# Attention and gated MoE on one core: transposes of q and x through the DMA crossbar, batch loads held behind them, and a regrouped opening

## The chip, the cores and the metric

The kernel runs on one core of a Trainium2 chip. The metric is the device time of one execution in microseconds (us). The core has five engines that run their own instruction streams in order and wait for each other through semaphores: TensorE (PE, matmuls and transposes, with its weight loads shown as PEld), VectorE (DVE), ScalarE (ACT), GpSimd (POOL) and SyncE (SP). SP and POOL also issue DMA transfers, each from its own queue. PSUM, where matmuls put their results, is used in 8 buffers, four for each of two pools.

## The reference

There are 8 batches of 8 heads, 576 tokens and 64 channels a head. Attention is linear, then normalised by head and token; the gated feed-forward block works on 4608 tokens of 512 channels, with 1536 hidden columns:

```python
kv = np.einsum('bhsd,bhse->bhde', k, v)
out = np.einsum('bhsd,bhde->bhse', q, kv)
rms = np.sqrt(np.mean(out * out, axis=-1, keepdims=True) + 1e-06)
x = (out / rms * g_norm)            # then [B, S, H*D] as 4608 x 512
g = x @ w_gate
gelu = 0.5 * g * (1.0 + erf(g * inv_sqrt2))
val = x @ w_val
ffn_out = gelu * val @ w_out
res_gate = 1.0 / (1.0 + np.exp(-(x @ w_res)))
return x + res_gate * ffn_out
```

## The kernel before, in words

Work goes by blocks. Blocks 0 to 7 hold the first 512 tokens of batches 0 to 7, as 4 groups (j) of 128 tokens; block 8 gathers the last 64 tokens of all batches, two batches to a group. All matmuls take fp16 and sum in fp32.

A MoE block has 12 slots of `m_gval` (one hidden tile f each: 4 matmuls `gps` with the gate weights, 4 matmuls `vps` with the value weights, N = 512, then gelu on ACT and the product `hid` on DVE) and 4 slots of `m_out` (one group j each: 4 matmuls `rps` for the gate of the residual, 12 matmuls `fps` over the hidden tiles, then `pf` and `osb` on DVE and a store from SP). Both `gps` and `vps` need x with its channels on the partitions, the tile `xT`; `m_out` adds x itself, the tile `t`. Block 0 is in another form: its first two hidden tiles are made group by group while the attention of batch 0 is finished, and its outputs run over f for all four groups at once (`out_by_f`).

The attention of batch b = m + 1 is woven into the slots of block m, by the table in `attn_plan`: `by_token` (L106, DVE) puts q and k into token order; `a_qT` transposes q with 16 PE transposes (L151) that ACT copies out of PSUM (L152); `a_kv` makes k'v with 20 matmuls (L161, L168); `a_o` makes the output with 16 matmuls (L190); ACT squares it (L183), DVE sums (L184), `a_norm` finds 1/rms on DVE, `a_t` (L248) scales into `t`; `a_xT` transposes that with 16 PE transposes (L260) which ACT copies out with the factor g (L261); `a_x` (L267, DVE) multiplies `t` itself by g. Odd batches also do the last 64 tokens of two batches: 4 more transposes of q (`a_rem_qT`, L200), `a_rem_o`, and 4 more of x. Six of the seven such batches, 2 to 7, run in blocks 1 to 6; the attention of batch 1 runs in block 0.

`load_batch` issues six cast transfers (fp32 in HBM to fp16 in SBUF) on POOL's queue. Its call stands in the second slot of a block, and the transfer of q waits until `by_token` has read the buffer. The order on each engine is the order in which the program calls; nothing is rescheduled.

The opening loads q, k and v of batch 0 as fp32 in two halves of four heads on SP's queue, casts them on ACT, DVE and POOL, and runs the attention of batch 0 by half (`f_...` functions). `keep_warm` issues matmuls on zeros, whose result is not used. The weights follow on POOL's queue.

Of the kernel before, what the change touches and what calls it, by code (L numbers as in the profile page):

```python
# [18 lines left out]
def kernel(  # L19
# [15 lines left out]
    nc = tc.nc  # L35
# [96 lines left out]
    def new_block(blk):  # L132
        pool, kw = (xp, {}) if blk < B else (consts, {})
        t_t[blk] = pool.tile([P, NJ, C], FP16, tag="t" if blk < B else "tl", name="t")
        xT_t[blk] = pool.tile([P, NP, NJ * P], FP16, tag="xT" if blk < B else "xTl", name="xT")
# [119 lines left out]
    def a_xT(b, j):  # L255

        blk, jj = where(b, j)
        ps = pattn.tile([P, NP, P], FP16, tag="at", name="xtp")
        for cc in range(NP):
            nc.tensor.transpose(ps[:, cc, :], t_t[blk][:, jj, cc * P : (cc + 1) * P], ident)  # L260
        nc.scalar.activation(  # L261
            out=xT_t[blk][:, :, jj * P : (jj + 1) * P], in_=ps, func=AF.Copy, scale=gcol
        )

    def a_x(b, j):
        blk, jj = where(b, j)
        nc.vector.tensor_tensor(out=t_t[blk][:, jj, :], in0=t_t[blk][:, jj, :], in1=g16, op=ALU.mult)  # L267

# [14 lines left out]
    def m_mm(ps, ws, f, blk, j0, j1):  # L283
        w = w_of(ws, f)
        for cc in range(NP):
# [3 lines left out]
                rhs=xT_t[blk][:, cc, j0 * P : j1 * P],  # L289
                start=(cc == 0),  # L290
                stop=(cc == NP - 1),
# [11 lines left out]
    def m_gval_first(blk, after):  # L303

        hids[blk] = hidp.tile([P, NF, NJ * P], FP16, tag="hid", name="hid")
        tiles = [pmoe.tile([P, NJ * P], FP32, tag="mm", name=n) for n in ("gps", "vps", "gps", "vps")]
        for j in range(NJ):
            after(j)
            for f in range(2):
                m_mm(tiles[2 * f], wg_c, f, blk, j, j + 1)  # L310
                m_mm(tiles[2 * f + 1], wv_c, f, blk, j, j + 1)
        for f in range(2):
            m_act(blk, f, tiles[2 * f], tiles[2 * f + 1])

    def m_res(blk, j):
        rps = pmoe.tile([P, C], FP32, tag="mm", name="rps")
        for cc in range(NP):
            nc.tensor.matmul(  # L318
                rps,
                lhsT=xT_t[blk][:, cc, j * P : (j + 1) * P],  # L320
# [58 lines left out]
    for which in "kv":  # L379
        t = hidp.tile([P, NF, NJ * P], FP16, tag="hid", name=which + "f")  # L380
        t = t.rearrange("p a b -> p (a b)").bitcast(FP32)[:, 0 : H * NJ * D]
        raw[0, which] = t.rearrange("p (h x) -> p h x", h=H)
    for half in range(2):
        lo, hi = half * HH, (half + 1) * HH
        for which, t in (("q", q), ("k", k), ("v", v)):
            nc.sync.dma_start(out=raw[0, which][:, lo:hi, :], in_=rows4(t, 0, lo, hi))
# [5 lines left out]
    load_last_kv(0)  # L392
    ident32 = consts.tile([P, P], FP32, name="ident32")
    make_identity(nc, ident32)

# [34 lines left out]
    def f_cast(which, half, copy):  # L430
        hs = slice(half * HH, (half + 1) * HH)
        dst, src = b16_t[0, which], raw[0, which]
        if which == "v":
            copy(out=dst[:, hs, :], in_=src[:, hs, :])  # L434
        else:
            copy(
                out=dst.rearrange("p j h d -> p h j d")[:, hs, :, :],
                in_=src.rearrange("p h (j d) -> p h j d", j=NJ)[:, hs, :, :],
            )
# [55 lines left out]

    def f_t(half, j0, n):
        hs = slice(half * HH, (half + 1) * HH)
        ps = first["o", half, j0]
        nc.vector.reciprocal(out=rinv0[:, j0 : j0 + n, hs], in_=rms0[:, j0 : j0 + n, hs])
# [8 lines left out]
    def f_xT(half, j0, n, pool, tag):  # L508
        first["xT", half, j0] = ps = pool.tile([P, 2, n, P], FP16, tag=tag, name="xtp")
# [4 lines left out]

    def f_xT_out(half, j0, n, on_vector):
        ps = first["xT", half, j0]
        dst = xT0[:, 2 * half : 2 * half + 2, j0 * P : (j0 + n) * P].rearrange("p c (j t) -> p c j t", j=n)
# [6 lines left out]
    f_cast("q", 0, nc.scalar.copy)  # L524
    f_cast("k", 0, nc.vector.tensor_copy)
    f_qT(0)
    f_qT_out(0, nc.scalar.copy)
    f_qT_out(1, nc.vector.tensor_copy)
    f_cast("v", 0, nc.gpsimd.tensor_copy)
    keep_warm(3)  # L530
    f_kv(0)
    f_kv_out(0)
    f_cast("q", 1, nc.scalar.copy)
    f_o(0, 0, 2, pmoe, "mm")
    f_o(0, 2, 2, pmoe, "mm")
    f_sq(0, 0, 2)
    f_red(0, 0, 2)
    f_qT(1)
    f_qT_out(2, nc.scalar.copy)
    f_qT_out(3, nc.vector.tensor_copy)  # L540
    f_cast("k", 1, nc.gpsimd.tensor_copy)
    for i in range(len(WCS)):
        load_wgv(i)
    load_qr(0)
    f_sqrt(0, 0, 2)
    f_t(0, 0, 2)
    f_sq(0, 2, 2)
    f_red(0, 2, 2)
    f_sqrt(0, 2, 2)
    keep_warm(8)  # L550
    f_cast("v", 1, nc.vector.tensor_copy)
# [3 lines left out]
    f_xT_out(0, 0, 2, False)  # L555
    f_t(0, 2, 2)
    for j in range(NJ):
        f_o(1, j, 1, pattn, "at")
    f_sq(1, 0, 1)
    f_sq(1, 1, 1)  # L560
    f_red(1, 0, 1)
    f_sqrt(1, 0, 1)
    f_t(1, 0, 1)
    keep_warm(2)
    f_xT(0, 2, 2, pmoe, "mm")
    f_sq(1, 2, 1)
    f_xT(1, 0, 1, pattn, "at")
    f_xT_out(1, 0, 1, False)
    f_red(1, 1, 1)
    f_sqrt(1, 1, 1)  # L570
    f_t(1, 1, 1)
    f_xT_out(0, 2, 2, False)
    f_sq(1, 3, 1)
    f_red(1, 2, 1)

    def first_chunk(j):

        if j == 1:
            f_xT(1, 1, 1, pattn, "at")
            f_xT_out(1, 1, 1, False)  # L580
            f_sqrt(1, 2, 1)
            f_t(1, 2, 1)
            f_red(1, 3, 1)
        elif j == 2:
            f_xT(1, 2, 1, pattn, "at")
            f_sqrt(1, 3, 1)
            f_xT_out(1, 2, 1, False)
            f_t(1, 3, 1)
            nc.scalar.preload_act_table_set("gelu_and_others")
        elif j == 3:  # L590
            f_xT(1, 3, 1, pattn, "at")
            f_xT_out(1, 3, 1, True)

            nc.vector.memset(ones16, 1.0)
            nc.vector.tensor_copy(out=grow16, in_=grow[:, None, :].to_broadcast([1, H, D]))
            for t in last_kv[1]:
                nc.vector.memset(t[R:P], 0.0)
            for t in qtr:
                nc.vector.memset(t, 0.0)
# [8 lines left out]
    def attn_plan(b):  # L608
        odd = b % 2 == 1
# [3 lines left out]
        y = [lambda j=j: a_x(b, j) for j in range(NJ + 1)]  # L613
        return [
            [lambda: by_token(b, "q"), lambda: by_token(b, "k")],
            [lambda: attn_begin(b), lambda: a_qT(b, 0)] + ([lambda: load_batch(b + 1)] if b + 1 < B else []),
            [lambda: a_qT(b, 1), lambda: a_kv(b, 0, 2)],
            [lambda: a_kv(b, 2, 4)] + ([lambda: a_rem_qT(b)] if odd else []),
            [o[0]] + ([lambda: a_rem_o(b)] if odd else []),
            [o[1]],  # L620
            [o[2]],
            [o[3]],
            [lambda: a_norm(b), t[0], t[1]],
            [t[2], t[3]],
            [t[4]] if odd else [],
            [],
            [x[0], x[1]],
            [x[2], x[3], y[0], y[1]],
            ([x[4]] if odd else []) + [y[2], y[3]],
            [y[4]] if odd else [],  # L630
        ]

    late = []
    for blk in range(B + 1):
        plan = {}
# [28 lines left out]
        if blk == 0:  # L664
            late = stores
# [30 lines left out]
```

## Time and profile before

| | |
|---|---|
| Time, median of 3 runs | 375.41 us (374.79 to 377.87) |
| The profiled execution | 375.42 us, of which the span of instructions is 373.6 us |
| Mean granted TensorE clock | 0.993 |
| PE busy | 358.0 us, 96% of the span |
| DVE, ACT, POOL busy | 215.6, 153.2 and 47.0 us |
| HBM read, written | 38.80 MB, 9.44 MB |
| Issue of a 512 KB batch load of q, k, v to its landing, median | 6.0, 7.9 and 9.8 us |

In rows of the profile, `L260 PE MATMUL xtp<-ident,t` is line 260 of the kernel before, on PE, which writes tile xtp and reads ident and t. A time in brackets is how long the engine sat idle before the row, and behind the arrow stands what ended that. Matmuls are pipelined, so the busy time of one (0.38 us at N = 512) is longer than the distance from one to the next; the distance is read from the starts in the timeline. In rows of windows, the columns are the window, its length, the busy time of PE, PEld, DVE, ACT and POOL with the number of instructions, the granted clock, the mean busy share of the DMA engines, and GB/s.

### The profile page before, as it was taken

Reading aid. Unit: us, or ns where it says so; the run is one execution under the profiler, and the core shown is the slowest. Engines: PE = TensorE matmul, PEld = TensorE weight load, DVE = VectorE, ACT = ScalarE, POOL = GpSimd, SP = SyncE. Lnnn points to the kernel's source line nnn. Section 1 sums busy time; section 2 is a strip of 40 time slices with the busy share of each in tenths; the row PEclk is TensorE's granted clock in tenths of the full one; section 3 lists DMA queues with packets and bytes.
Section 4 is the critical chain, followed back from the end, with each engine's and each line's share of the span. In section 5 each row is a group of like instructions: output and inputs, shape, how many; then the busy total and the mean of one; then the engine's idle time right before and its main releaser. Section 6 shows DMA issues by size and latency. Waiting matters only on the chain.

```text
span 373.6 us, 5442 instructions
## 1 busy us (share of the span) xinstructions
PE 358.0 (96%) x2120; PEld 180.6 (48%) x2120; DVE 215.6 (58%) x427; ACT 153.2 (41%) x257; POOL 47.0 (13%) x65
## 2 busy tenths in 40 slices
PE   6779999999999999999999999999999999999993
PEld 2554464554455455545464445444644444444441
DVE  2566448778546946584657664756478453343422
ACT  3563373453346344544364335533563333123310
POOL 3843140500050002200130005000000000000000
PEclk9899999999999999999999999999999999999998
DMA  9999997590159012901192029601000200020013
GB/s 246 187 202 197 198 200 74 81 221 2 58 107 141 0 56 63 182 5 56 61 172 18 28 84 133 58 31 56 30 0 2 84 29 2 28 80 7 0 43 70
DMA packets 49452, 30.76 MB, mean 82 GB/s; under 512 B 14098, under 2 KB 44818, under 8 KB 49426
## 3 DMA queue, kind: packets, MB, share of 16 engines
q0 software_dynamic: 40848, 17.83, 38.2%
q1 hardware_dynamic: 8578, 12.59, 9.6%
q8 instruction: 16, 0.26, 0.3%
q14 instruction: 10, 0.08, 0.1%
HBM read 38.80 MB, written 9.44 MB: 129 GB/s over the span
## 4 chain that ended last, share of the span: by engine, by line
PE 90%; DVE 5%; DMA 2%; ACT 1%; issue 1%; SPq 0%; DVEq 0%
PE gps L286 25%; PE vps L286 24%; PE fps L331 24%; PE rps L318 8%; DMA qf<-in_q_dram 2%; PE xtp L260 2%; PE kvp L161 2%; PE qtp L151 2%; PE op L190 2%; DVE t L501 1%; DVE pf L337 1%; DVE ss L485 1%; ACT xT L521 1%; PE orp L208 0%; PE kvp L168 0%
## 5 line engine op out<-in xcount | busy, mean ns | idle before, releaser
L286 PE MATMUL gps<-xT,wg 128*128 128x512 f16 (+1 forms) x456 | 112.6, 368 | 2.0 <-ACT xT L521 1.5
L275 DVE TENSOR_TENSOR hid<-ge,vps 128x512 f16<-128x512 f16 x108 | 73.6, 685 | 68.0 <-PE vps L286 67.8
L286 PE MATMUL vps<-xT,wv 128*128 128x512 f16 (+1 forms) x456 | 111.9, 368 | 0.0
L274 ACT ACTIVATE ge<-gps 128x512 f16<-128x512 f32 x108 | 64.5, 598 | 99.7 <-PE gps L286 92.9
L331 PE MATMUL fps<-wo,hid 128*128 128x512 f16 x432 | 99.6, 379 | 0.0
L286 PEld LDWEIGHTS <-wv 128*128 128x128 f16 x456 | 43.6, 98 | 50.2 <-issue 0.2
L331 PEld LDWEIGHTS <-hid 128*128 128x128 f16 x432 | 42.0, 98 | 49.3
L286 PEld LDWEIGHTS <-wg 128*128 128x128 f16 x456 | 41.8, 98 | 42.7 <-issue 2.6
L337 DVE SCALAR_TENSOR_TENSOR pf<-th,fps 128x512 f32<-128x512 f32 x36 | 24.5, 688 | 59.4 <-PE fps L331 59.4
L318 PE MATMUL rps<-wr,xT 128*128 128x512 f16 x144 | 36.9, 379 | 0.1
L327 ACT ACTIVATE th<-rps 128x512 f32<-128x512 f32 x36 | 21.5, 598 | 37.7 <-PE rps L318 37.7
L261 ACT ACTIVATE xT<-xtp,gcol 128x512 f16<-128x512 f16 x32 | 20.5, 685 | 37.6 <-PE xtp L260 37.6
L99 POOL DMA_DIRECT2D qraw<-in_q_dram x7 | 6.3, 894 | 162.0 <-DVE q L106 126.8
L342 DVE SCALAR_TENSOR_TENSOR osb<-pf,t 128x512 f32<-128x512 f32 x36 | 24.9, 691 | 1.1
L184 DVE TENSOR_REDUCE ss<-sq 128x8 f32<-128x512 f32 x32 | 21.9, 686 | 5.5 <-ACT sq L183 3.0
L183 ACT ACTIVATE sq<-op 128x512 f32<-128x512 f32 x28 | 16.8, 598 | 12.0 <-PE op L190 12.0
L318 PEld LDWEIGHTS <-xT 128*128 128x128 f16 x144 | 13.2, 98 | 13.9 <-issue 1.5
L248 DVE TENSOR_TENSOR t<-op,ny 128x512 f16<-128x512 f32 x28 | 17.9, 683 | 0.3
L152 ACT COPY qT<-qtp 128x1024 f16<-128x1024 f16 x14 | 14.2, 1013 | 9.1 <-PE qtp L151 9.1
L161 PE MATMUL kvp<-v,k 128*128 128x128 f16 x128 | 10.9, 222 | 3.3 <-POOL v L434 2.2
L267 DVE TENSOR_TENSOR t<-t,g 128x512 f16<-128x512 f16 x36 | 13.5, 418 | 0.0
L190 PEld LDWEIGHTS <-qT 128*128 128x128 f16 x112 | 8.6, 98 | 6.6
(82 smaller groups left out, 203.4 us busy)
## 6 DMA issues: line engine op xcount, KB each, us to landing
out_dram<-osb SPq DMA_DIRECT2D x32, 256.0 KB, 2.3
qraw<-in_q_dram POOLq DMA_DIRECT2D x7, 512.0 KB, 6.0
kraw<-in_k_dram POOLq DMA_DIRECT2D x7, 512.0 KB, 7.9
v<-in_v_dram POOLq DMA_DIRECT2D x7, 512.0 KB, 9.8
wo<-in_moe_w_out_dram POOLq DMA_DIRECT2D x3, 512.0 KB, 13.8
qf<-in_q_dram SPq DMA_DIRECT2D x2, 512.0 KB, 7.6
kf<-in_k_dram SPq DMA_DIRECT2D x2, 512.0 KB, 6.5
vf<-in_v_dram SPq DMA_DIRECT2D x2, 512.0 KB, 7.8
```

The costliest lines, as they stand in the source:

```text
L161: nc.tensor.matmul(ps, lhsT=k16[:, j, cs], rhs=v16[:, 2 * pr : 2 * pr + 2, j * D : (j + 1) * D], start=(j == 0), stop=False,)
L184: nc.vector.tensor_reduce(out=st[b]["ss"][:, j, :], in_=sq, op=ALU.add, axis=mybir.AxisListType.X)
L248: nc.vector.tensor_tensor(out=t_t[blk][:, jj, :].rearrange("p (h d) -> p h d", h=H), in0=s["o"][j].rearrange("p (h d) -> p h d", h=H), in1 ...
L261: nc.scalar.activation(out=xT_t[blk][:, :, jj * P : (jj + 1) * P], in_=ps, func=AF.Copy, scale=gcol)
L274: nc.scalar.activation(out=ge, in_=gps, func=AF.Gelu)
L275: nc.vector.tensor_tensor(out=hids[blk][:, f, :], in0=ge, in1=vps, op=ALU.mult)
L286: nc.tensor.matmul(ps[:, j0 * P : j1 * P], lhsT=w[:, cc, :], rhs=xT_t[blk][:, cc, j0 * P : j1 * P], start=(cc == 0), stop=(cc == NP - 1),)
L318: nc.tensor.matmul(rps, lhsT=xT_t[blk][:, cc, j * P : (j + 1) * P], rhs=wr16[:, cc, :], start=(cc == 0), stop=(cc == NP - 1),)
L327: nc.scalar.activation(out=th, in_=rps, func=AF.Tanh, scale=0.5)
L331: nc.tensor.matmul(fps, lhsT=hids[blk][:, f, j * P : (j + 1) * P], rhs=wo16[:, f, :], start=(f == 0), stop=(f == NF - 1))
L337: nc.vector.scalar_tensor_tensor(out=pf, in0=th, scalar=1.0, in1=fps, op0=ALU.add, op1=ALU.mult)
L342: nc.vector.scalar_tensor_tensor(out=osb, in0=pf, scalar=0.5, in1=t_t[blk][:, j, :], op0=ALU.mult, op1=ALU.add)
```

## The change

**Transposes.** For batches 2 to 7, q and x are transposed by DMA instructions with the transpose flag, issued on SP, from SBUF to SBUF: `d_qT` and `d_xT` (128x16x128 elements each), and for odd batches `d_rem_qT` and a second `d_xT` (128x4x128). Their PE transposes and the ACT copies behind them are gone; only the two small copies of `rem_qT_copy` remain. Since the factor g is no longer applied in an ACT copy, `a_x` now runs before the transpose of x. Tile `xT` has its groups outside its channels: a `gps` or `vps` matmul reads four pieces of 128 elements in place of 512 in a row.

**Placing.** `by_token`, `attn_begin` and `d_qT` of a batch move into the last slots of the block before (for batch 2 into slots 2 and 3 of block 1). `a_norm` and `a_t` move by a slot or two, and `a_x` with `d_xT` stands in the first `m_out` slot. Batch 1 keeps its PE transposes, in a plan of its own.

**Loads.** `load_behind` on POOL copies one element of `qT` (and of `qrT`) before it issues the load of the next batch, so that POOL waits there until the transposes of q have landed.

**Opening.** v of batch 0 comes in by two cast transfers on POOL's queue with no cast after them; the other casts are dealt out anew; the second half of attention is done for two groups at a time; and the first two hidden tiles take channels 0 to 255 for all four groups first (8 matmuls with N = 512) and then channels 256 to 511 group by group. The weights of the residual gate are loaded ahead of batch 1, and the calls of `keep_warm` come to 33 matmuls in place of 23.

```diff
@@ new_block
-        xT_t[blk] = pool.tile([P, NP, NJ * P], FP16, tag="xT" if blk < B else "xTl", name="xT")
+        xT_t[blk] = pool.tile([P, NJ, NP, P], FP16, tag="xT" if blk < B else "xTl", name="xT")
...
+    def d_qT(b):
+        nc.sync.dma_start(
+            out=st[b]["qT"].rearrange("p j c t -> p (j c) t"),
+            in_=b16_t[b, "q"].rearrange("p j h d -> p (j h d)"),
+            transpose=True,
+        )
+
+    def d_rem_qT(b):
+        st[b]["qrT"] = attnp.tile([P, NP, P], FP16, tag="qrT", name="qrT")
+        nc.sync.dma_start(out=st[b]["qrT"], in_=qr_t[b // 2], transpose=True)
+
+    def rem_qT_copy(b):
+        nc.scalar.copy(out=qtr[0][:, :, 0:R], in_=st[b]["qrT"][:, :, 0:R])
+        nc.scalar.copy(out=qtr[1][:, :, R : 2 * R], in_=st[b]["qrT"][:, :, R : 2 * R])
+
+    def d_xT(b, j0, j1):
+        blk, k0 = where(b, j0)
+        k1 = k0 + j1 - j0
+        nc.sync.dma_start(
+            out=xT_t[blk][:, k0:k1, :, :].rearrange("p j c t -> p (j c) t"),
+            in_=t_t[blk][:, k0:k1, :].rearrange("p j c -> p (j c)"),
+            transpose=True,
+        )
...
-    def m_mm(ps, ws, f, blk, j0, j1):
+    def m_mm(ps, ws, f, blk, j0, j1, c0=0, c1=NP):
         w = w_of(ws, f)
-        for cc in range(NP):
+        for cc in range(c0, c1):
             nc.tensor.matmul(
                 ps[:, j0 * P : j1 * P],
                 lhsT=w[:, cc, :],
-                rhs=xT_t[blk][:, cc, j0 * P : j1 * P],
+                rhs=xT_t[blk][:, j0:j1, cc, :],
...
-        for which, t in (("q", q), ("k", k), ("v", v)):
-            nc.sync.dma_start(out=raw[0, which][:, lo:hi, :], in_=rows4(t, 0, lo, hi))
+        for which, t in (("q", q), ("k", k)):
+            nc.sync.dma_start(out=raw[0, which][:, lo : lo + HH, :], in_=rows4(t, 0, lo, lo + HH))
+
+    def load_v0(lo):
+        nc.gpsimd.dma_start(out=b16_t[0, "v"][:, lo : lo + HH, :], in_=rows4(v, 0, lo, lo + HH))
+
+    load_v0(0)
...
-    load_last_kv(0)
     ident32 = consts.tile([P, P], FP32, name="ident32")
     make_identity(nc, ident32)
+    load_last_kv(0)
+    load_v0(HH)
...
+    def first_gval():
+        hids[0] = hidp.tile([P, NF, NJ * P], FP16, tag="hid", name="hid")
+        tiles = [pmoe.tile([P, NJ * P], FP32, tag="mm", name=n) for n in ("gps", "vps", "gps", "vps")]
+        for f in range(2):
+            m_mm(tiles[2 * f], wg_c, f, 0, 0, NJ, 0, 2)
+            m_mm(tiles[2 * f + 1], wv_c, f, 0, 0, NJ, 0, 2)
+        for j in range(NJ):
+            f_xT(1, j, 1, pattn, "at")
+            f_xT_out(1, j, 1, j == NJ - 1)
...
+            for f in range(2):
+                m_mm(tiles[2 * f], wg_c, f, 0, j, j + 1, 2, NP)
+                m_mm(tiles[2 * f + 1], wv_c, f, 0, j, j + 1, 2, NP)
...
+    def load_behind(b):
+        nc.gpsimd.tensor_copy(out=hold, in_=st[b]["qT"][0:1, 0, 0, 0:1])
+        if b % 2 == 1:
+            nc.gpsimd.tensor_copy(out=hold, in_=st[b]["qrT"][0:1, 0, 0:1])
+        load_batch(b + 1)
...
+    def plan_attn(b):
+        odd = b % 2 == 1
+        m = b - 1
+        begin = [lambda: by_token(b, "k"), lambda: attn_begin(b), lambda: d_qT(b)]
+        if odd:
+            begin.append(lambda: d_rem_qT(b))
+        if b == 2:
+            at(m, 2, lambda: by_token(b, "q"))
+            at(m, 3, *begin)
+            k0, o0, n0 = 4, 6, 10
+        else:
+            at(m - 1, NF + 1, lambda: by_token(b, "q"))
+            at(m - 1, NF + 2, *begin)
+            k0, o0, n0 = 1, 3, 7
+        at(m, k0, lambda: a_kv(b, 0, 2))
+        at(m, k0 + 1, lambda: a_kv(b, 2, 4))
+        if b + 1 < B:
+            at(m, k0 + 1, lambda: load_behind(b))
+        if odd:
+            at(m, k0 + 1, lambda: rem_qT_copy(b))
+            at(m, o0, lambda: a_rem_o(b))
+        for j in range(NJ):
+            at(m, o0 + j, lambda j=j: a_o(b, j))
+        at(m, n0, lambda: a_norm(b))
+        n0 += 1 if b == 2 else 2
+        for j in range(NJ):
+            at(m, n0 + j // 2, lambda j=j: a_t(b, j))
...
+        for j in range(NJ):
+            at(m, NF, lambda j=j: a_x(b, j))
+        at(m, NF, lambda: d_xT(b, 0, NJ))
+        if odd:
+            at(m, NF + 1, lambda: a_x(b, NJ), lambda: d_xT(b, NJ, NJ + 1))
```

How the rows stand on three engines, before and after. On SP, from the last store of block 0 to the fourth store of block 1 (osb is the output tile of one group; the numbers only tell buffers apart). Before:

```order
L347 DMA out_0_dram<-osb_934 128x512
L347 DMA out_0_dram<-osb_1126 128x512
L347 DMA out_0_dram<-osb_1163 128x512
L347 DMA out_0_dram<-osb_1202 128x512
L347 DMA out_0_dram<-osb_1229 128x512
```

After, at the same place:

```order
L360 DMA out_0_dram<-osb_861 128x512
L360 DMA out_0_dram<-osb_1078 128x512
L288 DMA_TRANSPOSE xT_791<-t_790 128x16x128
L360 DMA out_0_dram<-osb_1110 128x512
L360 DMA out_0_dram<-osb_1136 128x512
L271 DMA_TRANSPOSE qT_1140<-q16_915 128x16x128
L279 DMA_TRANSPOSE qrT_1144<-qr_602 128x4x128
L360 DMA out_0_dram<-osb_1168 128x512
```

The transpose of x (batch 2) has come in behind the first of the four stores, and those of q (batch 3) behind the third.

On DVE, the four `m_out` slots of block 2, in which batch 3 is the one on its way (t is x before and after the factor g). Before:

```order
L337 SCALAR_TENSOR_TENSOR pf<-th,fps 128x512
L342 SCALAR_TENSOR_TENSOR osb<-pf,t 128x512
L337 SCALAR_TENSOR_TENSOR pf<-th,fps 128x512
L342 SCALAR_TENSOR_TENSOR osb<-pf,t 128x512
L267 TENSOR_TENSOR t<-t,g_141 128x512 x2
L337 SCALAR_TENSOR_TENSOR pf<-th,fps 128x512
L342 SCALAR_TENSOR_TENSOR osb<-pf,t 128x512
L267 TENSOR_TENSOR t<-t,g_141 128x512 x2
L337 SCALAR_TENSOR_TENSOR pf<-th,fps 128x512
L342 SCALAR_TENSOR_TENSOR osb<-pf,t 128x512
L267 TENSOR_TENSOR t<-t,g_141 128x512
```

After:

```order
L350 SCALAR_TENSOR_TENSOR pf<-th,fps 128x512
L355 SCALAR_TENSOR_TENSOR osb<-pf,t 128x512
L267 TENSOR_TENSOR t<-t,g_140 128x512 x4
L350 SCALAR_TENSOR_TENSOR pf<-th,fps 128x512
L355 SCALAR_TENSOR_TENSOR osb<-pf,t 128x512
L267 TENSOR_TENSOR t<-t,g_140 128x512
L106 COPY q_1237<-qraw 128x8x4x64
L350 SCALAR_TENSOR_TENSOR pf<-th,fps 128x512
L355 SCALAR_TENSOR_TENSOR osb<-pf,t 128x512
L106 COPY k_1238<-kraw 128x8x4x64
L350 SCALAR_TENSOR_TENSOR pf<-th,fps 128x512
L355 SCALAR_TENSOR_TENSOR osb<-pf,t 128x512
```

All four products with g now stand in the first slot, and the reordering of q and k of batch 4 has moved up into the second and third from the block that follows.

On ACT, the end of the opening, from the first copy of x out of PSUM (xtp) to the loading of the gelu table. Before:

```order
L521 ACTIVATE xT<-xtp,gcol 128x2x256
L482 ACTIVATE sq<-op 128x256 x2
L494 ACTIVATE rms_154<-ss,eps_col 128x4
L482 ACTIVATE sq<-op 128x256
L521 ACTIVATE xT<-xtp,gcol 128x2x128
L494 ACTIVATE rms_154<-ss,eps_col 128x4
L521 ACTIVATE xT<-xtp,gcol 128x2x256
L482 ACTIVATE sq<-op 128x256
L521 ACTIVATE xT<-xtp,gcol 128x2x128
L494 ACTIVATE rms_154<-ss,eps_col 128x4 x2
L521 ACTIVATE xT<-xtp,gcol 128x2x128
L589 ACT_TABLE_LOAD
```

After:

```order
L544 ACTIVATE xT<-xtp,gcol 128x2x2x128
L495 ACTIVATE sq<-op 128x512 x2
L544 ACTIVATE xT<-xtp,gcol 128x2x2x128
L507 ACTIVATE rms_153<-ss,eps_col 128x2x4 x2
L544 ACTIVATE xT<-xtp,gcol 128x256 x3
L609 ACT_TABLE_LOAD
```

The squares and roots are done for two groups at a time and stand ahead of the three copies of single groups, which now follow each other.

229 lines of the change are left out of this document (111 added, 118 removed).

## The prediction

> **What bounds the kernel now.** I read the busy times first, then the chain of waits.
>
> ```profile
> PE 358.0 (96%) x2120; PEld 180.6 (48%) x2120; DVE 215.6 (58%) x427; ACT 153.2 (41%) x257; POOL 47.0 (13%) x65
> PE 90%; DVE 5%; DMA 2%; ACT 1%; issue 1%; SPq 0%; DVEq 0%
> ```
>
> PE is busy for 358.0 of 373.6 us, and 90% of the chain that ended last is PE. Windows cut at the starts of blocks show where it is not busy:
>
> ```profile
> 10.00:26.55 16.55, 11.65 (x130) 8.74 (x128) 10.21 (x29) 9.74 (x22) 11.24 (x14) 0.90 1.10 186
> 44.24:64.78 20.54, 19.36 (x150) 10.72 (x149) 13.62 (x33) 11.24 (x19) 4.70 (x6) 1.00 1.10 150
> 103.69:143.07 39.38, 39.38 (x246) 20.35 (x244) 25.13 (x49) 18.39 (x31) 4.69 (x6) 1.00 0.45 73
> 143.07:181.50 38.43, 38.43 (x230) 19.44 (x229) 24.13 (x48) 16.19 (x26) 4.70 (x6) 1.00 0.47 73
> 367.80:373.60 5.80, 0.09 (x1) 0.00 (x0) 1.38 (x2) 0.00 (x0) 0.00 (x0) 0.83 0.28 66
> ```
>
> The first row is the opening, the second the end of block 0, then block 2 (batch 3, odd) and block 3 (batch 4, even), then the tail, which the change leaves alone. In the blocks PE has no idle time at all, so each PE instruction taken out there shortens the run by its own distance, as long as its replacement is in time.
>
> **The transposes taken out.** Counts after 64 us, that is, for batches 2 to 7, and the small ones of all odd batches:
>
> ```profile
> L260 PE MATMUL xtp<-ident,t x108: 219/219/219, 92.4 to 295.2; 128*128 128x128 f16 x108
> L151 PE MATMUL qtp<-ident,q x96: 219/219/229, 68.7 to 265.3; 128*128 128x128 f16 x96
> L200 PE MATMUL qtrp<-ident,qr 128*128 128x128 f16 x16 | 1.5, 219 | 0.0
> 131.59 0.61 PE L260 MATMUL xtp<-ident,t 128*128 128x128 f16 x8
> 132.04 1.03 PE L318 MATMUL rps<-wr,xT 128*128 128x512 f16 x4
> 135.49 0.61 PE L260 MATMUL xtp<-ident,t 128*128 128x128 f16 x8
> ```
>
> 108 + 96 + 12 of the 16 small ones (batch 1 keeps 4) make 216. Eight occupy 132.04 - 131.59 = 0.45 us of PE, so one 0.056 us, and 216 of them 12.1 us. The ACT copies that vanish beside them lie on an engine that is busy 41%; I count nothing for them. The same rows give the length of an `m_out` slot without transposes: 135.49 - 132.04 = 3.45 us.
>
> **Waits in blocks 0 and 1.** PE's idle times there, in brackets, with what ended them:
>
> ```profile
> 45.85 0.62 PE L151 MATMUL qtp<-ident,q 128*128 128x128 f16 x8 [0.30 <-DVE q L106]
> 59.52 0.40 PE L260 MATMUL xtp<-ident,t 128*128 128x128 f16 x4 [0.43 <-DVE t L248]
> 60.12 0.40 PE L260 MATMUL xtp<-ident,t 128*128 128x128 f16 x4 [0.20 <-DVE t L248]
> 68.72 0.62 PE L151 MATMUL qtp<-ident,q 128*128 128x128 f16 x8 [0.32 <-DVE q L106]
> ```
>
> These are 1.25 us. The last transpose is gone; for the others batch 1's new plan leaves more slots between DVE's step and PE's (`by_token` at slots 11 and 12 and `a_qT` at 15; `a_t` at 20 and `a_xT` at 25). I take 1.0 us, between 0 and 1.25.
>
> **The room for the new transposes.** x of the next batch is needed at the first `gps` of the next block. DVE's steps before it, and the slot length:
>
> ```profile
> 128.01 1.28 DVE L248 TENSOR_TENSOR t<-op,ny 128x512 f16<-128x512 f32 x2
> 131.86 0.69 DVE L337 SCALAR_TENSOR_TENSOR pf<-th,fps 128x512 f32<-128x512 f32 x1 [0.78 <-PE fps L331]
> 132.59 0.69 DVE L342 SCALAR_TENSOR_TENSOR osb<-pf,t 128x512 f32<-128x512 f32 x1
> 137.09 0.75 DVE L267 TENSOR_TENSOR t<-t,g 128x512 f16<-128x512 f16 x2
> 143.07 1.03 PE L286 MATMUL gps<-xT,wg 128*128 128x512 f16 x4
> 144.79 1.03 PE L286 MATMUL gps<-xT,wg 128*128 128x512 f16 x4
> ```
>
> Behind the first `m_out` slot (PE's end 131.59) `osb` ends 1.69 us later, four products with g take about 1.5 more, so SP issues `d_xT` 3.2 us after that slot. Three slots of 3.45 us remain: room 10.35 - 3.2, about 7.2 us. Batch 2 has two `a_t` (1.28 us for two) ahead of it: 5.9. For q: `d_qT` is issued some 1.7 us after the third `m_out` slot (behind the store in SP's queue); until the first `a_o` PE has one `m_out` slot, four hidden tiles of 144.79 - 143.07 = 1.72 us, and 20 `kvp` of 0.056: 11.5 - 1.7 = 9.8 us. For batch 2, issued in block 1's slot 3 behind a late store, I get 5.5 us. The odd batches' small q transpose rides behind in the same room.
>
> The trace has no crossbar transpose, so its time T (512 KB, issue to landing) must be bounded:
>
> ```profile
> 0.74 0.45 SPq L386 DMA_DIRECT2D qf<-in_q_dram  x1
> 4.66 1.04 ACT L436 CAST q<-qf 128x1024 f16<-128x1024 f32 x1 [2.64 <-DMA qf<-in_q_dram]
> out_dram<-osb SPq DMA_DIRECT2D x32, 256.0 KB, 2.3
> qf<-in_q_dram SPq DMA_DIRECT2D x2, 512.0 KB, 7.6
> v<-in_v_dram POOLq DMA_DIRECT2D x7, 512.0 KB, 9.8
> ```
>
> From SP's queue, 512 KB with nothing ahead of it landed in 3.9 us (0.74 to 4.66); 256 KB out of SBUF takes 2.3. With three transfers ahead it took 7.6, and a v behind q and k of its batch 9.8. Below 2.3 is excluded, since half the bytes take that as a plain copy. Above there is no sure bound; 9.8 is the longest usual row. I take 3.9 to 5.5, near the row that stands alone: `load_behind` keeps the batch load out until q has landed, x is issued after the previous load is over, and only one 256 KB store runs beside each. At that T no transpose is late, and this term is 0. In general, with T between 7.2 and 9.8, the lateness is 5 (T - 7.2) + (T - 5.9) + (T - 5.5) = 7T - 47.4.
>
> Queued behind these transposes on SP are the stores; there are three `osb` buffers, and a store late by T still lands before its buffer's turn three slots (10.35 us) later. On POOL the load of the next batch queues behind `load_behind`. It starts when q lands, about a block before `by_token` needs it (for batch 3, about 17 us); q's load takes 6.0 and v's 9.8. So the hold costs nothing, unless T is above 15.
>
> **xT in four pieces.** No row has a 512-wide operand in pieces. The nearest:
>
> ```profile
> L161 PE MATMUL kvp<-v,k 128*128 128x128 f16 x128 | 10.9, 222 | 3.3 <-POOL v L434 2.2 <-DVE v L434 1.1
> L168 PE MATMUL kvp<-vl,kl 128*128 128x128 f16 x32 | 7.1, 223 | 0.0
> ```
>
> L161 reads two pieces of 64, L168 one of 128, both in about 222 ns. I take 0; at most, if each piece cost as much as a matmul of its own, 4 x 56 - 216 = 8 ns on some 850 matmuls, 6.8 us.
>
> **The opening.**
>
> ```profile
> 9.48 0.38 PE L161 MATMUL kvp<-v,k 128*128 128x128 f16 x4 [2.19 <-POOL v L434]
> 15.95 0.38 PE L161 MATMUL kvp<-v,k 128*128 128x128 f16 x4 [1.15 <-DVE v L434]
> 21.43 0.28 PE L286 MATMUL gps<-xT,wg 128*128 128x128 f16 x2
> 23.20 0.27 PE L286 MATMUL gps<-xT,wg 128*128 128x128 f16 x2
> 26.55 1.02 PE L286 MATMUL gps<-xT,wg 128*128 128x512 f16 x4
> DMA to landing us min/median/max: 7.3/7.3/7.3
> ```
>
> Both halves of `kvp` waited for casts of v (2.19 and 1.15 us) that no longer exist, and a round of the first tiles takes 23.20 - 21.43 = 1.77 us, because roots and products of each group stand inside it; with these done ahead I put a round at 1.3 us. Against that stand four channel-half steps of two matmuls each (1.7 us, the same PE work as before), and the last rows of v (`vl`, the 7.3 us row), which now stand behind the first half of v and the making of the identity on POOL (put at 2 us) and can hold the first `kvp` until 11. Walking engine by engine, the third hidden tile starts between 24.0 and 26.8 us in place of 26.55: a gain of 2.5 to -0.3. I take 1.2.
>
> This gain has to pass the loads:
>
> ```profile
> 33.26 0.76 POOL L125 DMA_DIRECT2D wo<-in_moe_w_out_dram x1
> 38.25 0.74 POOL L125 DMA_DIRECT2D wo<-in_moe_w_out_dram x1 [1.89 <-DMA kraw<-in_k_dram]
> DMA to landing us min/median/max: 13.8/13.8/13.9
> 51.36 1.03 PE L331 MATMUL fps<-wo,hid 128*128 128x512 f16 x4
> ```
>
> The last third of the output weights lands at 52.1, the first, issued at 33.26, at 47. In the new order all of batch 1's attention input stands ahead of `fps`, and PE reaches it near 48. That just fits.
>
> **The sum.** 12.1 + 1.0 + 1.2 = 14.3 us off the profiled execution's 375.42 us (span 373.6 and 1.8 around it), which agrees with the median of the runs, 375.41: **361.1 us**.
>
> **Rivals.**
>
> *Mildly late transposes.* T is 7.6, the row of a transfer with others ahead. Then 7 x 7.6 - 47.4 = 5.8 us come back: 366.9. For it: up to two transposes and a store share SP's queue. Against: 7.6 was seen under a full queue, and these windows have a DMA share of 0.45.
>
> *Transposes that become the bound: slower.* The gain is gone at 7T - 47.4 = 14.3, T = 8.8 us. At the row of 9.8 it is 21.2 us of waits: 375.4 - 14.3 + 21.2 = 382.3, with PE idle at the first `gps` of blocks 2 to 7. For it: `vl`, 64 KB in rows of 64 fp16 values, took 7.3 us in the opening, so that pieces and not bytes can set a transfer's time, and the crossbar may work in pieces too. Against: the room was 7.2 us in every block but one, and DMA is idle half the time. On this the Trainium skill ("VectorE: DVE Perf Modes", The three transpose paths) gives 1309 ns for a 128x128 block by the crossbar against 390 on TensorE; sixteen in a row would be an estimated 20.9 us, far past 8.8. Its page "DMA: Bandwidth & Descriptors" (Latency and other measured facts) gives 261 GB/s for such transposes, an estimated 2.0 us for 512 KB. No row of this trace decides between them; the PE row here, 0.056 us apart, shows only that the 390 is not what PE pays in this kernel.
>
> *Pieces cost.* The 6.8 us above: 367.9, seen in the distance of `gps` matmuls.
>
> *The opening gives nothing.* Weights or `vl` hold it: 362.3, inside the range of the forecast.
>
> **Chances.** Forecast, with the last case, 0.62; mildly late 0.16; slower 0.16; pieces 0.06. A difference of 1% (3.75 us) is what a measurement here can tell from none. Faster by more: the first, the pieces and nearly all of the second (T below 8.3): 0.81. Same: T from 8.3 to 9.3, 0.06. Slower: 0.13. The range begins at 358.0 (all gains at their upper end, 15.9, give 359.5, and 1.5 for the walk of the opening) and ends at 370.0, past the second and fourth cases; left out is the slower case and a few hundredths.
>
> **What would show it.** PE should have 230 fewer matmuls (216 fewer transposes, 24 fewer in the first tiles, 10 more to keep warm). Blocks 2 and 3 should last 37.1 and 36.6 us. If transposes are late, the first `gps` of a block waits for DMA xT, or `op` for DMA qT, and the issue rows give T; a landing above 7.2 us makes the forecast wrong, above 8.8 its sign. Distances of `gps` above 216 ns would show the pieces, `fps` waiting for wo the loads.

## The result, and the profile after

The changed kernel took 363.01 us in the median of four runs (361.17 to 363.92), the kernel before 376.0 us on the same chip (four runs, 374.79 to 377.87). The ratio is 0.9644, 95% interval 0.9586 to 0.9702. The profiled execution took 361.17 us (span 359.4 us), the one before 375.42: 14.25 us apart, where the medians are 13.0 apart. The first experiment shows how two executions of the changed kernel come to differ.

The busy times and the chain that ended last in the changed kernel:

```profile
PE 345.9 (96%) x1890; PEld 167.9 (47%) x1890; DVE 213.2 (59%) x422; ACT 124.6 (35%) x214; POOL 48.5 (14%) x73
...
PE 92%; DMA 2%; DVE 2%; ACT 1%; issue 1%; POOL 0%; DVEq 0%; POOLq 0%
```

PE has 2120 - 1890 = 230 fewer matmuls and is still 96% busy: the kernel is shorter, not bound by something else. ACT lost 28.6 us of busy time, an engine that PE hardly waits for. The DMA transposes, in the rows of DMA issues (count, median us from issue to landing; the row of xT holds three small ones):

```profile
xT<-t SPq DMA_TRANSPOSE x9, 4.3
qT<-q SPq DMA_TRANSPOSE x6, 4.5
qrT<-qr SPq DMA_TRANSPOSE x3, 2.7
```

So T, which the trace of before could not give, is 4.3 to 4.5 us in the median; single transposes of 512 KB took 4.3 to 5.1. The largest waits of PE behind the first matmul (us in total, times, longest):

```profile
PE kvp L168 <- DMA vl<-in_v_dram: 3.0, 1, 3.0
PE gps L311 <- ACT xT L544: 1.7, 3, 0.6
...
PE gps L311 <- DVE xT L542: 0.4, 1, 0.4
```

No matmul waits for a DMA transpose, and all these waits lie in the opening. The timeline of PE, in the opening and at the starts of blocks 1, 2, 3 and 7:

```profile
8.58 0.38 PE L161 MATMUL kvp<-v,k 128*128 128x128 f16 x4 [0.42 <-DMA v<-in_v_dram]
...
11.93 0.22 PE L168 MATMUL kvp<-vl,kl 128*128 128x128 f16 x1 [2.97 <-DMA vl<-in_v_dram]
...
22.19 0.27 PE L311 MATMUL gps<-xT,wg 128*128 128x128 f16 x2 [0.56 <-ACT xT L544]
...
23.47 0.27 PE L311 MATMUL gps<-xT,wg 128*128 128x128 f16 x2 [0.56 <-ACT xT L544]
...
26.87 1.02 PE L311 MATMUL gps<-xT,wg 128*128 128x512 f16 x4 [0.35 <-ACT ge L299]
27.73 1.03 PE L311 MATMUL vps<-xT,wv 128*128 128x512 f16 x4
...
63.47 1.02 PE L311 MATMUL gps<-xT,wg 128*128 128x512 f16 x4
...
100.32 1.03 PE L311 MATMUL gps<-xT,wg 128*128 128x512 f16 x4
...
137.31 1.03 PE L311 MATMUL gps<-xT,wg 128*128 128x512 f16 x4
...
284.38 1.03 PE L311 MATMUL gps<-xT,wg 128*128 128x512 f16 x4
```

The start of block 7 in the timeline of the kernel before:

```profile
298.66 1.03 PE L286 MATMUL gps<-xT,wg 128*128 128x512 f16 x4
```

Windows of the changed kernel over its opening and blocks 2 and 3 (columns as in the prediction):

```profile
10.00:26.87 16.87, 12.16 (x114) 7.62 (x114) 7.89 (x21) 8.73 (x18) 11.04 (x15) 1.00 1.32 192
100.32:137.31 36.99, 36.99 (x205) 18.10 (x204) 25.15 (x50) 13.41 (x24) 5.05 (x8) 1.00 0.68 113
137.31:173.85 36.54, 36.54 (x197) 17.64 (x196) 23.73 (x47) 11.95 (x20) 4.88 (x7) 1.00 0.65 106
```

The account, before against after, from the starts of blocks:

| stretch | before | after | gain |
|---|---|---|---|
| to the third hidden tile | 26.55 | 26.87 | -0.3 |
| from there to block 1 | 38.23 | 36.60 | 1.6 |
| blocks 1 to 6 | 233.88 | 220.91 | 13.0 |
| block 7 to the end of the span | 74.9 | 75.0 | -0.1 |

In blocks 2 and 3 PE is as full as before (36.99 of 36.99), with fewer instructions. The opening gave nothing. From 10 us on to the tail it is the one stretch in which PE idles for more than some tenths of a us: 4.7 of 16.9.

### The profile page after: what moved, and what is told of

Same layout as the page of the kernel before. It is cut to its first block, busy times and chain, and to the rows that moved or that the text cites. A ratio compares the mean times of both kernels' runs of the same rounds, so it can differ in the third digit from the quotient of the medians.

```text
span 359.4 us, 4974 instructions
## 1 busy us (share of the span) xinstructions
PE 345.9 (96%) x1890; PEld 167.9 (47%) x1890; DVE 213.2 (59%) x422; ACT 124.6 (35%) x214; POOL 48.5 (14%) x73
## 4 chain that ended last, share of the span: by engine, by line
PE 92%; DMA 2%; DVE 2%; ACT 1%; issue 1%; POOL 0%; DVEq 0%; POOLq 0%
PE gps L311 26%; PE fps L344 26%; PE vps L311 25%; PE rps L331 9%; DMA vl<-in_v_dram 2%; PE kvp L161 2%; PE op L190 2%; PE kvp L168 1%; PE orp L208 1%; PE xtp L532 0%; ACT xT L544 0%; PE idle L436 0%; DVE ss L498 0%; ACT xT L261 0%; DVE osb L355 0%
## 5 line engine op out<-in xcount | busy, mean ns | idle before, releaser
L331 PEld LDWEIGHTS <-xT 128*128 128x128 f16 x144 | 14.1, 98 | 17.0
L665 POOL COPY hold<-qT 1x1 f16<-1x1 f16 x5 | 0.9, 177 | 141.0 <-DMA qT<-q 141.0
L161 PEld LDWEIGHTS <-k 128*128 128x128 f16 x128 | 8.9, 98 | 5.8 <-issue 1.9
L436 PE MATMUL idle<-zeros 128*128 128x512 f16 x33 | 10.3, 456 | 1.2 <-DVE zeros L414 1.2
```

The costliest lines, as they stand in the source:

```text
L161: nc.tensor.matmul(ps, lhsT=k16[:, j, cs], rhs=v16[:, 2 * pr : 2 * pr + 2, j * D : (j + 1) * D], start=(j == 0), stop=False,)
L331: nc.tensor.matmul(rps, lhsT=xT_t[blk][:, j, cc, :], rhs=wr16[:, cc, :], start=(cc == 0), stop=(cc == NP - 1),)
```

## The experiments

### The changed kernel again

The changed kernel without any edit, so that the edits below have their own reference.

> The changed kernel as it is, on the same chip as the three that follow, so that each is compared with it and not only with the kernel before. Expected: 0.964 of the kernel before, crossbar transposes of 512 KB landing in 4.3 to 4.5 us, the third hidden tile of block 0 starting at 26.9 us.

Measured: 362.96 us (362.04 to 364.0), ratio 0.9673 (0.9644 to 0.9702); span of the profiled execution 360.7 us. It is 1.3 us longer than the span above, and the timeline of PE has that difference complete when the third hidden tile starts:

```profile
28.20 1.02 PE L311 MATMUL gps<-xT,wg 128*128 128x512 f16 x4 [0.35 <-ACT ge L299]
```

against 26.87. The wait for `vl` is the same in both (2.95 and 2.97 us). What differs is the granted clock behind it. These are the windows of this run that hold most of the wait and what follows it:

```profile
9.60:13.01 3.41, 1.03 (x10) 0.73 (x11) 0.42 (x1) 0.00 (x0) 3.41 (x5) 1.00 1.46 205
13.01:16.43 3.42, 3.42 (x21) 2.22 (x20) 2.24 (x5) 2.10 (x5) 3.42 (x6) 0.50 1.28 164
```

In the profile of the section above the clock was 1.00 from 10 to 20 us. So the opening differs between executions of one program, and the profile shown there has the best one seen: in the next experiment, which leaves the opening alone, the clock is halved from 11.08 to 17.91 us and the third hidden tile starts at 29.72.

### The transposes back on TensorE

```diff
-        begin = [lambda: by_token(b, "k"), lambda: attn_begin(b), lambda: d_qT(b)]
+        begin = [lambda: by_token(b, "k"), lambda: attn_begin(b), lambda: a_qT(b, 0), lambda: a_qT(b, 1)]
...
-            at(m, NF, lambda j=j: a_x(b, j))
-        at(m, NF, lambda: d_xT(b, 0, NJ))
+            at(m, NF + j // 2, lambda j=j: a_xT(b, j))
+            at(m, NF + 1 + j // 2, lambda j=j: a_x(b, j))
```

The small transposes of the odd batches go back in the same way, and the two `hold` copies are gone. Opening, plan of batch 1 and layout of `xT` stay as changed.

> The changed kernel with the transposes of q and x of batches 2 to 7 given back to TensorE, with their ACT copies, at about the slots where the crossbar transposes are issued, and with no hold; opening, layout of xT and the plan of batch 1 stay. Theory A (the gain is PE time of the 216 transposes): 12.1 us longer than the changed kernel, blocks 2 and 3 at 39.3 and 38.4 us again. Theory B (a good part of the gain comes from the new opening and the new plan): less than 9 us longer.

Measured: 374.13 us (372.43 to 375.41, ten runs), ratio 0.9965 (0.9945 to 0.9984). That is 11.2 us above the changed kernel by the medians. In the profiles, blocks 1 to 6 run between these rows of PE:

```profile
66.32 1.02 PE L311 MATMUL gps<-xT,wg 128*128 128x512 f16 x4
...
298.98 1.03 PE L311 MATMUL gps<-xT,wg 128*128 128x512 f16 x4
```

232.66 us against 220.91: 11.75 us for 216 matmuls, 0.054 each. Nearly the whole gain is the transposes leaving PE. Everything else of the change together is worth 0.35% by this ratio (0.16 to 0.55), about 1.3 us. The blocks are the firmer of the two comparisons, since the medians also hold the openings, which differ by up to 2.85 us between the profiles (26.87 to 29.72).

### Without the hold

```diff
 def load_behind(b):
-        nc.gpsimd.tensor_copy(out=hold, in_=st[b]["qT"][0:1, 0, 0, 0:1])
-        if b % 2 == 1:
-            nc.gpsimd.tensor_copy(out=hold, in_=st[b]["qrT"][0:1, 0, 0:1])
         load_batch(b + 1)
```

> The two one-element copies on POOL are left out, so the load of the next batch is issued as soon as its buffers are free, which is when q and k of the batch before have been put in order: at the moment when the transpose of q is issued. Theory A (the hold is what keeps the transposes short): the transpose of q shares the DMA engines with 3 MB of loads and lands in 8 us or more; batch 2, with a room of 5.5 us, is then 2.5 us or more late, and batches 3 to 7, with 9.8 us, some 0 to 5 us each, so the run is 3 to 25 us longer than the changed kernel. Theory B (the transposes are short by themselves): landing below 5.5 us, no PE wait, the same time within 0.3%.

Measured: 405.36 us (401.24 to 406.8), ratio 1.0784 (1.0721 to 1.0848): 42.4 us above the changed kernel, and slower than the kernel before. The landing fits theory A (8 us or more); the loss is well above its 3 to 25 us. The rows of DMA issues in this run:

```profile
xT<-t SPq DMA_TRANSPOSE x9, 4.3
qT<-q SPq DMA_TRANSPOSE x6, 14.2
qrT<-qr SPq DMA_TRANSPOSE x3, 9.8
```

The spread for tile qT alone, and the waits of PE:

```profile
DMA to landing us min/median/max: 5.6/14.2/17.4
```

```profile
PE orp L208 <- ACT qtr L282: 16.9, 2, 9.5
PE op L190 <- DMA qT<-q: 15.5, 3, 8.7
```

The transposes of x, which are issued ahead of a batch load (for batch 3 at 106.69, 2.2 us before it), take 4.3 us as before. Those of q take 14.2 in place of 4.5. The timelines of POOL, SP and PE show it for batch 3:

```profile
108.88 0.89 POOL L99 DMA_DIRECT2D qraw<-in_q_dram  x1 [30.34 <-DVE q L106]
...
111.49 8.59 SPq L271 DMA_TRANSPOSE qT<-q  x1
...
120.19 2.52 SPq L279 DMA_TRANSPOSE qrT<-qr  x1
...
130.47 1.23 PE L208 MATMUL orp<-kv,qtr 128*128 128x128 f16 x8 [9.49 <-ACT qtr L282]
```

The load is issued 2.6 us ahead of the transpose; the issue of the transpose alone then holds SP for 8.59 us (2.14 in the changed kernel), the small one queues behind it and lands 9.8 us after its issue, and PE stands for 9.49 us. The last transpose of q, batch 7, has no load behind it and landed in 5.6 us, the least of the six. The Trainium skill says ("DMA: Bandwidth & Descriptors", Issuing engines are not separate DMA queues) that transfers started from different engines run on the same 16 DMA engines and interleave; the trace agrees, with 14.2 us against 4.5. That the slowing is the sharing of the DMA engines, and not of something narrower on the way, no run here separates.

The waits are 32.4 us, 10 less than the loss. Where the rest is, the window behind the first of them shows (columns as before, the clock third from the end):

```profile
88.00:91.00 3.00, 3.00 (x11) 1.35 (x12) 1.02 (x2) 1.19 (x2) 0.00 (x0) 0.50 1.59 159
```

After 8.73 us of waiting TensorE was granted half its clock. So it was behind three of the other four waits (9.49, 7.46 and 4.29 us), and not behind the shortest (2.48). From the end of each of the four waits the half clock lasts 2.9 to 5.3 us, 16.2 in all, and half of that is lost: 8.1 us. With the 32.4 that makes 40.5 of 42.4 us. The start of block 0 has another 0.8: block 1 starts at 65.56, against 64.79 in the changed kernel's second profile. The next experiment has the same half clock.

### x transposed three times

In `d_xT`, ahead of each 512 KB transpose of x, SP transposes the same tile twice into a tile that nobody reads:

```diff
+        for _ in range(2 if j1 == NJ else 0):
+            nc.sync.dma_start(
+                out=spare.rearrange("p j c t -> p (j c) t"),
+                in_=t_t[blk][:, k0:k1, :].rearrange("p j c -> p (j c)"),
+                transpose=True,
+            )
         nc.sync.dma_start(
```

> Ahead of each 512 KB transpose of x (batches 2 to 7), two more of the same tile into a spare buffer are issued from SP, so that the one that is used is late by what two of them take on the queue. It measures the room: the prediction put it at 7.2 us (batch 2: 5.9). If transposes of one queue overlap (SP is busy some 1.9 us for each), x lands near 4.3 + 2 x 1.9 = 8.1 us after the first issue, and the first gps of blocks 2 to 7 waits about 0.9 us, of block 2 about 2.2: near 7 us more in all. If they run one after the other, x lands at 12.9 us and the waits are 5.7 us five times and 7 once: 35 us more. If the room is much wider than the prediction's 7.2 us, there is no wait.

Measured: 397.52 us (one run), span 395.7 us. The wait of PE that is new, then the timelines of SP and PE at the ends of blocks 1 and 2:

```profile
PE gps L317 <- DMA xT<-t: 23.6, 6, 4.8
```

```profile
95.26 5.97 SPq L289 DMA_TRANSPOSE spare<-t  x2
...
101.28 2.87 SPq L294 DMA_TRANSPOSE xT<-t  x1
...
106.33 1.89 PE L317 MATMUL gps<-xT,wg 128*128 128x512 f16 x4 [4.80 <-DMA xT<-t]
...
138.25 6.17 SPq L289 DMA_TRANSPOSE spare<-t  x2
...
149.36 1.89 PE L317 MATMUL gps<-xT,wg 128*128 128x512 f16 x4 [3.64 <-DMA xT<-t]
```

PE would have been ready at 106.33 - 4.80 = 101.53 for batch 2, 6.3 us after the first issue, and 7.5 us after it for batch 3 (149.36 - 3.64 - 138.25). These are the rooms that the prediction put at 5.9 and 7.2. Three transposes back to back take about 11 us to the last landing, 3 us of SP each: neither side by side nor one whole landing after another (3 x 4.3 = 12.9).

The loss against the changed kernel is 34.5 us by the medians, and the waits explain 23.6. The windows behind the waits ahead of blocks 2 and 3:

```profile
106.30:110.10 3.80, 3.77 (x9) 1.31 (x10) 0.07 (x1) 0.60 (x1) 0.00 (x0) 0.50 1.01 213
149.36:155.25 5.89, 5.89 (x14) 2.04 (x15) 0.69 (x1) 1.15 (x2) 0.21 (x2) 0.50 0.91 202
```

Five of the six waits (3.62 to 4.80 us) were followed by half the clock; one of 3.70 us was not. From the end of the wait it lasted 3.0 to 5.9 us, 22.2 in all, which costs 11.1 us, some 2 a time. With the waits that makes 34.7, against a loss of 34.5. That this is near the 35 us expected for transposes one after the other is chance: the waits alone are a third less.

Why one wait of six was spared, and why the openings differ, can be read from the moments at which the clock changes. Between two such moments of a run there is always a multiple of 3.41 us, so each run can be cut into periods of that length. In the ten traces, from 5 us on, a period at full clock in which PE idled for 2.19 us or more was followed by one at half clock; with 1.93 us or less it was followed by one at full clock, but for one period with 1.69 us (the run without the hold, at 22.74). A wait that falls across the end of a period can thus be longer and cost less:

| run, wait of PE | periods it falls in, from | PE idle in them | clock behind |
|---|---|---|---|
| kernel before, 2.19 us | 6.35 | 2.19 us | 0.50 |
| changed kernel, 2.97 us | 6.74 and 10.15 | 1.61 and 1.87 us | 1.00 |
| changed kernel again, 2.95 us | 6.19 and 9.60 | 1.33 and 2.38 us | 0.50 |
| x three times, 3.64 us | 145.01 | 2.70 us | 0.50 |
| x three times, 3.70 us | 230.34 and 233.76 | 1.93 and 1.77 us | 1.00 |

The Trainium skill ("TensorE: Matmul & The Clock Gate", What's actually happening) says that a whole idle window of about 3.4 us halves the clock and that the window runs freely, so that the moment matters. The traces agree on the length and on the moment; the window need not be idle as a whole, 2.19 of 3.41 us were enough.

### The order of the small loads in the opening

The wait of 2.97 us for `vl` suggested the order on POOL's queue.

```diff
+    load_last_kv(0)
     load_v0(0)
...
-    load_last_kv(0)
```

> Only the opening's order on POOL is changed: the last rows of k and v of batch 0 (64 KB each) are issued ahead of the first half of v, as in the kernel before, and not behind it. Theory A (the wait of 2.97 us for vl is what ate the opening's gain): the first kvp is over near 9.7 us in place of 12.2, the third hidden tile starts at 24.5 to 25.5 us in place of 26.9, and the run is 1.4 to 2.4 us shorter than the changed kernel. Theory B (the loads of the weights or another wait stands right behind): the third hidden tile starts within 0.5 us of 26.9, and the run is the same.

Measured: 363.18 us (362.15 to 364.03), ratio 0.9669 (0.9639 to 0.9699): no gain, and theory A fell. PE's timeline:

```profile
12.36 0.59 PE L161 MATMUL kvp<-v,k 128*128 128x128 f16 x4 [4.63 <-DMA v<-in_v_dram]
...
29.73 1.02 PE L311 MATMUL gps<-xT,wg 128*128 128x512 f16 x4 [0.35 <-ACT ge L299]
```

The wait moved from `vl` to v and grew to 4.63 us; whichever order they were issued in, the last of POOL's first transfers that PE needs landed near 12 us. The order was not the cause. The third hidden tile starts at 29.73, later than either theory had it, since in this execution the clock was halved from 11.21 to 18.04 us. That the transfers together are the cause, because they share the queue, is so far only an argument; the next experiment takes one of them off it.

### v of batch 0 as before

```diff
+        if lo == 0:
+            vf = stage.tile([P, HH, NJ * D], FP32, name="vf")
+            nc.sync.dma_start(out=vf, in_=rows4(v, 0, 0, HH))
...
-    load_v0(0)
+    load_last_kv(0)
...
-    load_last_kv(0)
...
-    keep_warm(6)
+    nc.gpsimd.tensor_copy(out=b16_t[0, "v"][:, 0:HH, :], in_=vf)
+    keep_warm(12)
```

The first half of v comes as fp32 on SP's queue again and is cast on POOL; the small rows come first on POOL's queue; six more warming matmuls fill the gap.

> Only the opening: the first half of v of batch 0 comes again as fp32 on SP's queue behind the first halves of q and k and is cast on POOL, the last rows of k and v are issued first on POOL, and 12 in place of 6 matmuls on zeros stand ahead of the first kvp. The second half of v stays a cast transfer. Theory A (what holds the first kvp is that three transfers on POOL's queue share it and end together near 12 us): the first kvp is at 9.5 us, as in the kernel before, the third hidden tile starts 1.5 to 2.4 us earlier than in the changed kernel, and so does the end. Theory B (SP's queue and POOL's share the same bytes, so that what v gains the second halves of q and k lose): within 0.5 us of the changed kernel.

Measured: 360.15 us (359.41 to 362.61, six runs), ratio 0.9595 (0.957 to 0.9619). PE's timeline:

```profile
9.60 0.38 PE L161 MATMUL kvp<-v,k 128*128 128x128 f16 x4 [0.53 <-POOL v L554]
...
18.92 0.61 PE L311 MATMUL vps<-xT,wv 128*128 128x512 f16 x2 [0.80 <-DMA wv<-in_moe_w_val_dram]
...
25.74 1.02 PE L311 MATMUL gps<-xT,wg 128*128 128x512 f16 x4 [0.35 <-ACT ge L299]
```

The wait for `vl` is gone, the clock is 1.00 throughout the opening, and the third hidden tile starts 1.1 us before the better profile of the changed kernel and 2.5 us before the other. Against the better one that is less than the 1.5 to 2.4 expected, and theory B has a share in it. The first `gps` starts 2.1 us earlier (17.53 against 19.62), but a new wait of 0.80 us for the value weights follows. POOL issues the weights behind its cast of the second half of q, and that half now comes 2 us later on SP's queue (the cast starts at 11.25 in place of 9.25, the first weights go out at 12.24 in place of 10.24). The edit changes the path of v, the order on POOL and the warming matmuls together; what each is worth alone was not run.

### Rounds one ahead

In the first two hidden tiles, the transpose and copy of group j + 1 are issued ahead of the matmuls of group j:

```diff
-        for j in range(NJ):
+        def ready(j):
             f_xT(1, j, 1, pattn, "at")
             f_xT_out(1, j, 1, j == NJ - 1)
...
+        ready(0)
+        for j in range(NJ):
+            if j + 1 < NJ:
+                ready(j + 1)
```

> Only the first hidden tiles: the transpose and copy of group j + 1 are issued ahead of the matmuls of group j. In the changed kernel PE waits 0.56, 0.56, 0.56 and 0.44 us for the copies. Expected: three of the four waits shrink to 0.2 us or less, the third hidden tile starts 1.0 to 1.5 us earlier, and the run is shorter by that. If the loads of the weights hold the opening, there is no gain.

Measured: 360.9 us (359.64 to 362.43, six runs), ratio 0.9603 (0.9574 to 0.9631), about 2 us under the changed kernel. PE's waits for `xT` fall from 2.1 us in four to the one in the first row; the second is the third hidden tile:

```profile
PE gps L311 <- ACT xT L544: 0.5, 1, 0.5
```

```profile
27.68 1.02 PE L311 MATMUL gps<-xT,wg 128*128 128x512 f16 x4 [0.86 <-ACT ge L299]
```

The wait for `ge` grows from 0.35 to 0.86 us. From the first `gps` to the third hidden tile it is 5.76 us (21.92 to 27.68), and 7.25 in both profiles of the changed kernel: 1.5 us less, the upper end of what was expected. That the tile does not start earlier than 26.87 comes from the clock, halved from 11.02 to 17.84 us in this execution.

### Both

The two edits together.

> The last two changes together. Theory A: their gains add, 2.5 to 3.9 us shorter than the changed kernel, near 359.5 us. Theory B: the start of block 0 is earlier, but PE then waits for the output weights or for the input of batch 1, and less than 1.5 us is left at the end.

Measured: **358.26 us** (357.64 to 360.59, six runs), ratio 0.9552 (0.9526 to 0.9578): 4.7 us under the changed kernel's 362.96, where the two edits alone gave 2.8 and 2.1, and faster than both kernels. That is theory A, with more than its 2.5 to 3.9 us. (The last three, and the run with x transposed three times, were on another chip than the changed kernel's repeat; the kernel before differs by 0.15 us between the two, 375.45 and 375.6.) The third hidden tile starts here:

```profile
23.88 1.02 PE L311 MATMUL gps<-xT,wg 128*128 128x512 f16 x4 [0.86 <-ACT ge L299]
```

This is 3.0 us ahead of the changed kernel's better opening, and at the lower end of the walk in the prediction (24.0). The wait for the value weights is not in this profile.

## Why the prediction was right, step by step

The forecast was 361.1 us, from 358.0 to 370.0; the median is 363.01, and the profiled execution, against which the sum was made, 361.17. The sum of 14.3 us was 14.25, but that it came so close is luck: two of its terms are off and cancel, and the profiled execution had the best opening. By the medians the gain is 13.0. The mechanism of the large term, the transposes, is shown.

**The transposes taken out** (12.1). The experiment that puts them back has 11.2 us by the medians and 11.75 over blocks 1 to 6. The distance of 0.056 us was the right row: a matmul taken out of a stretch where PE never waits is worth its distance, not its 0.219 us of busy time. Blocks 2 and 3, put at 37.1 and 36.6 us, last 36.99 and 36.54. Blocks 1 to 6 gained 13.0 against the 11.75, and the starts of single matmuls in the traces account for it. 216 transposes at 0.0558 us are 12.05. Gaps of 1.23 us in the blocks of the kernel before are gone: 0.48 at the last wait that the prediction listed (68.72) and 0.08 to 0.17 ahead of the first `rps` of each block. The changed kernel has a new gap of 0.30 ahead of `kvp` at 72.40, which the kernel with the transposes back on TensorE has not.

**Waits in blocks 0 and 1** (1.0). From the third hidden tile to block 1 it is 1.6 us, and with the 0.5 of block 1 less the new 0.3 some 1.8. That is above the range (to 1.25), and the reason is how the four waits were read. A time in brackets runs from the end of the matmul before, but the next could have started 0.16 us earlier (0.379 us of busy time against a distance of 0.216). From start to start the four cost 0.47, 0.59, 0.36 and 0.48, together 1.90 in place of 1.25. All four are gone; two more gaps that I had not listed (0.28 and 0.30) went, and small new ones (0.39) came.

**The opening** (1.2). This is the step that failed: it lost 0.3 us in one profile and 1.65 in the other (28.20), and 3.2 in a third with the same opening (29.72). The part on rounds was right (23.47 - 22.19 = 1.28 us, put at 1.3). The part on `vl` was named as a risk, "can hold the first `kvp` until 11", and it held until 11.93. I kept 1.2 between the bounds although that row decided against it: the first part of `kvp` was over near 10.2 us before and is over near 12.3 now. No bound had the clock in it, though the row of the opening before shows 0.90: the kernel before runs at half clock from 9.76 to 13.17 us, behind its wait of 2.19 us. The last experiments bear the cause out: with v off POOL's queue and more warming matmuls the term becomes a gain of 0.8, and with the rounds one ahead 2.7 (26.55 - 23.88).

**Late transposes** (0). T was assumed between 3.9 and 5.5 and is 4.3 to 5.1. The rooms hold too. In the changed kernel itself the timeline of SP shows the issue of x for batches 2 and 3:

```profile
94.21 1.85 SPq L288 DMA_TRANSPOSE xT<-t  x1
...
130.00 1.76 SPq L288 DMA_TRANSPOSE xT<-t  x1
```

From there to the starts at 100.32 and 137.31 are 6.1 and 7.3 us, put at 5.9 and 7.2. The rooms for q follow from the run without the hold, whose timelines of SP and PE have these rows:

```profile
73.37 6.73 SPq L271 DMA_TRANSPOSE qT<-q  x1
...
87.97 0.61 PE L190 MATMUL op<-kv,qT 128*128 128x128 f16 x4 [8.73 <-DMA qT<-q]
...
160.62 5.53 SPq L271 DMA_TRANSPOSE qT<-q  x1
...
174.41 0.61 PE L190 MATMUL op<-kv,qT 128*128 128x128 f16 x4 [4.29 <-DMA qT<-q]
```

87.97 - 8.73 - 73.37 = 5.9 us for batch 2 (put at 5.5) and 9.5 for batch 4 (9.8). The smallest room, 5.9 us, is 1.4 above the 4.5 that this transpose took, so this term did not hang on luck.

**The hold costs nothing.** True, and it is only half of the matter: I had the reason that T stays low ("keeps the batch load out until q has landed"), but did not price it. Without it T is 14.2 us and the kernel is slower than before.

**xT in four pieces** (0). From 26.87 to 27.73 four `gps` matmuls take 0.86 us, 0.215 each, as before. `fps` did not wait for wo.

**The rivals.** "Mildly late" and "transposes that become the bound" did not come, since T stayed below every room. The mechanism of the second is real, the run without the hold shows it; but its price was set too low. The formula 7T - 47.4 counts waits alone, and the runs put about 2 us of halved clock behind most waits above 2.2 us, so the break-even may lie below 8.8. The two figures of the Trainium skill that I set against each other are settled as far as they go: 16 blocks in a row at the 1309 ns of "VectorE: DVE Perf Modes" (The three transpose paths) would be an estimated 20.9 us, and 512 KB landed in 4.3 to 4.5. The 2.0 us estimated from the 261 GB/s of "DMA: Bandwidth & Descriptors" (Latency and other measured facts; the page gives it for transposes with a non-contiguous middle dimension) is nearer, and half of what was measured with issue and landing.

## What to carry to other kernels

Where TensorE is never idle, a transpose by DMA is worth the distance that its matmul takes on PE, as long as the time from its issue to its first reader is longer than its landing with everything that may run beside it. Keep large loads out of that time: a one-element copy that holds a load's queue cost nothing here and kept 42 us. And price a wait on TensorE with the clock behind it: a wait of some 2.2 us or more can cost about 2 us beyond itself, and whether it does depends on the moment at which it falls. Read the price of a wait from start to start, since the time in brackets leaves out the tail of the matmul before it.

## What the runs showed of the hardware

- A 512 KB transpose from SBUF to SBUF landed in 4.3 to 5.1 us in the changed kernel, and in 13.7 us (batch 4) and 17.4 us (batch 3) with a batch load of casts issued just ahead of it; SP is then held up to 8.59 us by the issue of one, in place of about 2.
- Back to back, three of them land in about 11 us, 3 us of SP each.
- With v's first half and the last rows of k and v issued first on POOL's queue, the last that PE needs lands between 11.9 and 12.9 us, in either order.
- The granted clock changes by periods of 3.41 us. PE idle for 2.19 us or more of one was followed by half the clock, 1.93 or less by the full clock, with one exception at 1.69. The opening of the changed kernel, not its blocks, differs by 1.3 us between its two profiles for this reason.
